# Seven of eight head groups put into one loop with register-based waits, in a decode-attention kernel that streams its cache

## Chip, cores, metric

One core of one Trainium2 chip. The metric is the device time of one execution in microseconds (us). The kernel before takes 1273.72 us (median of 3 runs, 1273.58 to 1274.66).

## The reference, cut to what matters

```python
# 16 query heads, 8 key/value heads, 65536 cached keys, head size 256, model width 448, bf16
g = sigmoid((x * gate_w).sum(-1, keepdims=True))
q = x @ wq                                            # one token
p = softmax((q @ k.T) * 256 ** -0.5)                  # two query heads share one K and V head
a = concat(p @ v) @ wo
b = gelu(layernorm(x)[:, None] * w1 + b1) @ w2 + b2   # the "mixer", 14 blocks of 128
out = g * a + (1 - g) * b
```

K and V are 268 MB each and are read once. Everything else is small. A *group* is one K/V head with its two query heads; there are eight.

## The kernel before, the parts that the change and the argument touch

A group is cut into six chunks of keys (6, 6, 5, 5, 5, 5 steps of 2048 keys). For each chunk one K load and one V load, of 5 or 6 MB, go into a ring of three slots. So the order of loads is K0, V0, K1, V1, ..., and a load waits until the slot of the third load before it is free. A K slot is free when VectorE has transposed it (`turn`); a V slot is free when TensorE has multiplied it (`p_v`).

```python
RING = 3
def load(item):                   # item 2*i is K of chunk i, 2*i+1 its V; i runs over all groups
    ...
    nc.sync.dma_start(out=ring[item % RING][...], in_=src[...])

n = 0
for i in range(total):            # total = 8 groups x 6 chunks, all unrolled
    g, c = divmod(i, n_chunks)
    for s in range(sizes[c]):
        turn(i, s, n)             # VectorE: transpose 2048 keys into kT (two buffers)
        scores(i, s, n)           # TensorE: 8 matmuls on kT
        mixer(n)                  # from step 4 on: one block per 8 steps, on ScalarE, POOL, TensorE
        if c == 0 and g > 0:      # the group before is finished inside the next one's first steps
            if s == 0: o_turn(g - 1) ...
            if s == 1: o_out(g - 1)
        n += 1
    load(2 * i + RING)            # into the K slot that turn has freed
    softmax(i)                    # ScalarE exp, VectorE transpose
    ...
    for s in range(...): p_v(i, s)
    load(2 * i + 1 + RING)        # into the V slot that p_v has freed
    if c == n_chunks - 1 and g + 1 < HKV:
        ...copy of pv; queries(g + 1)
# (cut) the tail: last chunk, output projection, store
```

The softmax here doesn't subtract the row's maximum and nothing guards it: scores larger than these inputs give would overflow.

## Time and profile before

| what | before |
|---|---|
| median time | 1273.72 us |
| DMA engines busy, slices at 90% or more | 39 of 40 |
| data moved | 545 MB, 429 GB/s on average |
| TensorE, VectorE busy | 58%, 49% |

The lines of the page of the kernel before: span, TensorE's busy time, the DMA engines' share and rate in 40 equal slices of the span, the DMA queues (packets, MB, share of 16 engines), and the loads (KB each, median us from issue to landing).

```profile
span 1271.5 us, 10502 instructions
PE 740.7 (58%) x4576; PEld 291.7 (23%) x4576; DVE 627.8 (49%) x388; ACT 58.4 (5%) x149; POOL 78.4 (6%) x145
...
DMA  9999999999999999999999999999999999999997
GB/s 409 424 428 434 432 437 431 430 433 432 434 428 436 433 433 432 431 435 431 432 432 432 435 432 432 433 430 435 433 430 436 432 432 432 434 426 439 435 426 308
...
q1 hardware_dynamic: 15416, 540.55, 98.6%
...
q8 instruction: 36, 0.59, 0.2%
...
ring<-in_A_k_cache_dram SPq DMA_DIRECT2D x31, 5120.0 KB, 30.0
ring<-in_A_v_cache_dram SPq DMA_DIRECT2D x31, 5120.0 KB, 23.5
```

The DMA engines are busy 90% or more in 39 of the 40 slices, so they are the limit. A 5 MB load needs about 12 us at 432 GB/s but lands 23.5 or 30.0 us after its issue: when it is issued, one to two others are still queued. Queue q8: 36 fetches of 16 KB of instructions.

The line of the table of waits (who waited, for whom, us in total, times, longest) that says the same from VectorE's side:

```profile
DVE kT L351 <- DMA ring<-in_A_k_cache_dram: 386.0, 46, 10.5
```

The boundary between groups seven and eight in the timeline (start, us, engine or issuing queue, line, operation, in brackets the idle time before it and who ended it): the K1 issue after the last p.v of group seven, VectorE's transposes of K0 of group eight, and the V1 issue that they free.

```profile
1120.18 0.33 SPq L97 DMA_DIRECT2D ring<-in_A_k_cache_dram  x1
...
1125.65 4.50 DVE L351 STREAM_TRANSPOSE kT<-ring 128x2048 f32<-128x2048 f32 x2 [8.16 <-DMA ring<-in_A_k_cache_dram]
...
1140.79 0.33 SPq L97 DMA_DIRECT2D ring<-in_A_v_cache_dram  x1
```

In the chain of waits, that K1 load and what it released:

```profile
1120.18 34.40 DMA ring<-in_A_k_cache_dram
...
1154.76 2.32 DVE kT L351
```

V1 is issued at 1140.8, while K1 is still landing until 1154.6: the queue is 14 us ahead.

### The profile page before, as it was taken

The numbers are of one execution on the slowest core, as the hardware profiler recorded it, in microseconds if no ns is written. First come the engines' busy times: TensorE is split into PE (matmuls) and PEld (weight loads), VectorE is DVE, ScalarE is ACT, GpSimd is POOL, SyncE is SP. The second block draws the span as 40 slices with busy tenths as digits, with TensorE's granted clock in tenths as the row PEclk, the third lists the DMA queues.
The fourth block names the chain that finished last, engine by engine and source line by source line (L and its number), as shares of the span: only waits on it lengthen the run. The fifth ranks groups of instructions, "written<-read, shape, count | busy, mean of one in ns | idle before, by whom it ended". The sixth has DMA issues, their size and how long they took to land.

```text
span 1271.5 us, 10502 instructions
## 1 busy us (share of the span) xinstructions
PE 740.7 (58%) x4576; PEld 291.7 (23%) x4576; DVE 627.8 (49%) x388; ACT 58.4 (5%) x149; POOL 78.4 (6%) x145
## 2 busy tenths in 40 slices
PE   1566556664566546665566646665466555665467
PEld 1222122221222212221222212222122211222123
DVE  2555354644545454553545445454454535544455
ACT  0000000000000000000000000000000000000000
POOL 4110101111011110110000000000000000000000
PEclk9878877887778877888778887788777887878889
DMA  9999999999999999999999999999999999999997
GB/s 409 424 428 434 432 437 431 430 433 432 434 428 436 433 433 432 431 435 431 432 432 432 435 432 432 433 430 435 433 430 436 432 432 432 434 426 439 435 426 308
DMA packets 16843, 544.92 MB, mean 429 GB/s; under 512 B 2202, under 2 KB 2332, under 8 KB 3484
## 3 DMA queue, kind: packets, MB, share of 16 engines
q1 hardware_dynamic: 15416, 540.55, 98.6%
q0 software_dynamic: 1376, 3.69, 0.8%
q8 instruction: 36, 0.59, 0.2%
q14 instruction: 11, 0.09, 0.0%
q10 hardware_dynamic: 4, 0.00, 0.0%
HBM read 544.22 MB, written 0.00 MB: 428 GB/s over the span
## 4 chain that ended last, share of the span: by engine, by line
DMA 62%; PE 19%; DVE 11%; issue 6%; ACT 1%; POOL 0%; DVEq 0%; ACTq 0%; SPq 0%; POOLq 0%
DMA ring<-in_A_k_cache_dram 59%; PE sc L359 14%; DVE kT L351 9%; PE pv L382 5%; DMA zb<-in_B_b_dram 2%; DMA ring<-in_A_v_cache_dram 1%; DVE pT L370 1%; ACT p L366 1%; PE den_ps L398 0%; PE misc L270 0%; PE acc L314 0%; DVEq L351 0%; PE misc L425 0%; PE misc L274 0%; DVE dsum L390 0%
## 5 line engine op out<-in xcount | busy, mean ns | idle before, releaser
L359 PE MATMUL sc<-kT,qw 128*128 128x512 bf16 x2048 | 587.8, 441 | 425.6 <-DVE kT L351 424.3
L351 DVE STREAM_TRANSPOSE kT<-ring 128x2048 f32<-128x2048 f32 x256 | 576.4, 2290 | 476.9 <-DMA ring<-in_A_k_cache_dram 386.0
L359 PEld LDWEIGHTS <-qw 128*128 128x128 bf16 x2048 | 218.9, 109 | 780.9 <-DVE kT L351 324.0
L382 PE MATMUL pv<-ring,pT 128*4 128x512 bf16 x2032 | 127.5, 401 | 61.8 <-DVE pT L370 61.8
L370 DVE STREAM_TRANSPOSE pT<-p 128x512 bf16<-128x512 bf16 x48 | 34.1, 711 | 130.9 <-ACT p L366 130.9
L382 PEld LDWEIGHTS <-pT 128*4 128x4 bf16 x2032 | 47.2, 90 | 136.3 <-DVE pT L370 81.7
L366 ACT ACTIVATE p<-sc 128x512 bf16<-128x512 f32 x48 | 28.7, 597 | 1035.1 <-PE sc L359 1035.1
L143 POOL DMA_DIRECT2D wo<-in_A_wo_dram x8 | 6.3, 790 | 552.5 <-PE acc L314 552.5
L333 POOL TENSOR_SCALAR t_b<-t_b 128x448 f32<-128x448 f32 x14 | 7.9, 564 | 224.9 <-ACT t_b L325 224.6
L336 POOL TENSOR_TENSOR t_b<-t_b,u_b 128x448 f32<-128x448 f32 x14 | 15.9, 1139 | 1.2
L343 POOL TENSOR_TENSOR gel<-t_b,u_b 128x448 bf16<-128x448 f32 x14 | 15.9, 1133 | 1.2
L339 POOL TENSOR_SCALAR t_b<-t_b,half_g 128x448 f32<-128x448 f32 x14 | 8.9, 636 | 106.4 <-ACT t_b L338 101.3
L414 PEld LDWEIGHTS misc<-sel,pvs 128*128 128x128 f32 x64 | 13.8, 299 | 3.6 <-issue 2.0
L414 PE MATMUL misc<-sel,pvs 128*128 128x2 f32 x64 | 12.2, 313 | 0.5 <-DVE pvs L472 0.5
L398 PE MATMUL den_ps<-pick,dsum 128*128 128x2 f32 x32 | 4.8, 256 | 12.5 <-DVE dsum L390 12.5
L227 PE MATMUL misc<-zb,one_f 1*128 1x2 f32 x2 | 0.6, 343 | 19.4 <-DMA zb<-in_B_b_dram 19.4
L325 ACT ACTIVATE t_b<-h_bc,b1T,w1T 128x448 f32<-128x448 f32 x14 | 10.5, 751 | 4.7 <-DVE h_bc L257 4.7
L329 POOL TENSOR_SCALAR u_b<-h_bc,w1T,b1T 128x448 f32<-128x448 f32 x14 | 10.0, 715 | 2.1 <-DVE qT L277 0.9
L366 ACT ACTIVATION_READ_ACCUMULATOR p<-sc 128x1 f32 x48 | 9.3, 194 | 0.0
L230 DVE TENSOR_SCALAR gate<-gate 128x2 f32<-128x2 f32 x1 | 0.2, 169 | 18.4 <-ACT gate L229 18.4
L164 POOL TENSOR_SCALAR_AFFINE_SELECT pick<-pick 128x2 f32<-128x2 f32 x44 | 8.5, 195 | 3.0 <-POOL pick L164 0.3
L338 ACT ACTIVATE t_b<-t_b 128x448 f32<-128x448 f32 x14 | 8.0, 572 | 13.4 <-POOL t_b L336 13.4
(75 smaller groups left out, 68.1 us busy)
## 6 DMA issues: line engine op xcount, KB each, us to landing
ring<-in_A_k_cache_dram SPq DMA_DIRECT2D x31, 5120.0 KB, 30.0
ring<-in_A_v_cache_dram SPq DMA_DIRECT2D x31, 5120.0 KB, 23.5
ring<-in_A_k_cache_dram SPq DMA_DIRECT2D x16, 6144.0 KB, 32.3
ring<-in_A_v_cache_dram SPq DMA_DIRECT2D x16, 6144.0 KB, 27.3
ring<-in_A_k_cache_dram SPq DMA_DIRECT2D x5, 1024.0 KB, 25.8
ring<-in_A_v_cache_dram SPq DMA_DIRECT2D x4, 1024.0 KB, 22.0
wo<-in_A_wo_dram POOLq DMA_DIRECT2D x8, 448.0 KB, 18.8
ring<-in_A_wq_dram SPq DMA_DIRECT2D x1, 3072.0 KB, 10.3
```

The lines of the kernel that those rows point to most:

```text
L164: nc.gpsimd.affine_select(out=t, in_=t, compare_op=ALU.not_equal, fill=1.0, base=-row, pattern=[[step, w]], channel_multiplier=1,)
L325: nc.scalar.activation(out=t_b[:], in_=h_bc[:], func=ACT.Square, scale=w1T[:, b:b + 1], bias=b1T[:, b:b + 1],)
L329: nc.gpsimd.tensor_scalar(out=u_b[:], in0=h_bc[:], scalar1=w1T[:, b:b + 1], scalar2=b1T[:, b:b + 1], op0=ALU.mult, op1=ALU.add,)
L336: nc.gpsimd.tensor_tensor(out=t_b[:], in0=t_b[:], in1=u_b[:], op=ALU.mult)
L339: nc.gpsimd.tensor_scalar(out=t_b[:], in0=t_b[:], scalar1=1.0, scalar2=half_g[:, 0:1], op0=ALU.add, op1=ALU.mult,)
L343: nc.gpsimd.tensor_tensor(out=gel[:], in0=t_b[:], in1=u_b[:], op=ALU.mult)
L351: nc.vector.transpose(out=kT[n % 2][:].bitcast(FP32), in_=kn[:, s * SB * 128:(s + 1) * SB * 128])
L359: nc.tensor.matmul(sc[i % 2][:], lhsT=qw[g % 2][:, q, PAD - s:PAD - s + 128], rhs=kv[:, :, q // 2, :, q % 2], start=(s == 0 and q == 0), s ...
L366: nc.scalar.activation(out=p_t[i % 2][:], in_=sc[i % 2][:], func=ACT.Exp, scale=scale, accum_out=den[g % 2][:, c:c + 1],)
L370: nc.vector.transpose(out=pT_t[i % 2][:], in_=p_t[i % 2][:])
L382: nc.tensor.matmul(pv[g % 2][32 * a:32 * a + 4, :], lhsT=pT[:, k, :, s], rhs=vt[:, j * DH:(j + 2) * DH], start=first and k < 4, stop=last ...
L414: nc.tensor.matmul(o_ps[:, 2 * c:2 * c + 2], lhsT=pvs[:, lo:lo + 128], rhs=sel[:, 2 * half:2 * half + 2], start=(half == 0 and c == 0), st ...
```

## The change

The intent: the eight groups are the same work, so seven become the body of one loop (a seventh of that code) and the eighth, with the special tail, stays unrolled. `iteration_sync="reg_based"` is chosen so that no barrier stands between passes. A group is finished at its own end and no longer inside the next one, `pv`, `den`, `qw` and `wo_t` need one buffer each, and the mixer moves into group eight, with two product buffers and a block per one and a half steps.

```diff
-    n = 0
-    for i in range(total):
-        g, c = divmod(i, n_chunks)
-        for s in range(sizes[c]):
-            turn(i, s, n)
-            scores(i, s, n)
-            mixer(n)
-            if c == 0 and g > 0:
-                ... (o_turn, o_out of the group before)
+    def group(g):
+        final = g is HKV - 1
+        n = 0
+        for i in range(n_chunks):
+            ends = i == n_chunks - 1
+            for s in range(sizes[i]):
+                turn(i, s, n)
+                scores(i, s, n)
+                if final:
+                    mixer(n)
+                n += 1
+            load(g, 2 * i + RING)        # items 12, 13, 14 are K0, V0, K1 of group g + 1
+            softmax(i)
+            ... den_sum, den_tot, p_v as before
+            load(g, 2 * i + 1 + RING)
+        if not final:
+            queries(g + 1)
+            nc.scalar.activation(out=pvs[:], in_=pv[:], func=ACT.Copy)
+            o_turn(); ...; o_out()
+            load_wo(g + 1)
+
+    with tc.For_i(0, HKV - 1, 1, iteration_sync="reg_based") as g:
+        group(g)
+    group(HKV - 1)
```

(The cut parts of the diff only pass `g` as a register into addresses and drop the double buffers.) The diff does not show what the built program does: at the loop's *exit*, SyncE waits 34.4 us, until the last load that the loop has issued has landed, and then all engines meet at a barrier before group eight: TensorE, VectorE, ScalarE and GpSimd all start on it between 1151.1 and 1151.3 us, after 32 to 40 us idle (parts of the trace are below).

More of the change, by code (lines that the diff above doesn't have):

```diff
@@ L64 @@
     n_chunks = len(sizes)
-    n_steps = HKV * sum(sizes)
+    n_items = 2 * n_chunks
+    assert n_items % RING == 0 and n_chunks % 2 == 0 and sum(sizes) % 2 == 0 and n_items > RING + 2
     scale = 1.0 / (DH ** 0.5)
@@ L80 @@
     sc = [psum.tile([128, 512], FP32, name=f"sc{i}") for i in range(2)]
-    pv = [psum.tile([128, 512], FP32, name=f"pv{i}") for i in range(2)]
+    pv = psum.tile([128, 512], FP32, name="pv")
     misc = psum.tile([128, 512], FP32, name="misc")
@@ L85, with piece @@
     acc = psum.tile([128, 512], FP32, name="acc")
-    total = HKV * n_chunks
-    def piece(item, j, n):
+    def piece(g, item, j, n):
         i, is_v = divmod(item, 2)
-        g, c = divmod(i, n_chunks)
-        nb = sizes[c] * SB
-        lo = sum(sizes[:c]) * SB * 128
-        src = (A_v_cache if is_v else A_k_cache)[0, g, lo:lo + 128 * nb, :]
-        src = src.rearrange("(p j) d -> p (j d)", j=nb)
+        nb = sizes[i] * SB
+        lo = sum(sizes[:i]) * SB * 128
+        src = (A_v_cache if is_v else A_k_cache)[0, bass.ds(g, 1), lo:lo + 128 * nb, :]
+        src = src.rearrange("o (p j) d -> p (o j d)", j=nb)
         nc.sync.dma_start(
@@ L99, in piece, with load @@
         )
-    def load(item):
+    def load(g, item):
         last = sizes[-1]
-        if item < 2 * total - 2:
-            piece(item, 0, sizes[item // 2 % n_chunks] * SB)
-        elif item == 2 * total - 1:
+        if item >= n_items:
+            if g is not HKV - 1:
+                load(g + 1, item - n_items)
+        elif g is not HKV - 1 or item < n_items - 2:
+            piece(g, item, 0, sizes[item // 2] * SB)
+        elif item == n_items - 1:
             for s in range(last):
-                piece(item - 1, s * SB, SB)
+                piece(g, item - 1, s * SB, SB)
             for s in range(last - 1):
-                piece(item, s * SB, SB)
-            piece(item, (last - 1) * SB, SB - TAIL)
-            piece(item, last * SB - TAIL, TAIL)
+                piece(g, item, s * SB, SB)
+            piece(g, item, (last - 1) * SB, SB - TAIL)
+            piece(g, item, last * SB - TAIL, TAIL)
     wq_slot = ring[RING - 1]
@@ L123 @@
     for item in range(RING - 1):
-        load(item)
+        load(0, item)
     x_row = const.tile([1, D], BF16)
@@ L138 @@
     nc.gpsimd.dma_start(out=zb[:, 1:2], in_=B_b2.rearrange("(o n) -> o n", o=1))
-    wo_t = [const.tile([128, 4, D], BF16, name=f"wo{i}") for i in range(2)]
+    wo_t = const.tile([128, 4, D], BF16)
     def load_wo(g):
-        nc.gpsimd.dma_start(
-            out=wo_t[g % 2][:],
-            in_=A_wo[g * 512:(g + 1) * 512, :].rearrange("(q p) n -> p q n", p=128),
-        )
+        src = A_wo.rearrange("(g q p) n -> p g q n", q=4, p=128)[:, bass.ds(g, 1)]
+        nc.gpsimd.dma_start(out=wo_t[:], in_=src.rearrange("p o q n -> p (o q) n"))
     ident = const.tile([128, 128], BF16)
@@ L185 @@
     pT_t = [work.tile([128, 512], BF16, name=f"pT{i}") for i in range(2)]
-    den = [work.tile([128, n_chunks], FP32, name=f"den{i}") for i in range(2)]
+    den = work.tile([128, n_chunks], FP32, name="den")
     dsum = work.tile([128, len(classes)], FP32, name="dsum")
@@ L195 @@
     qr = const.tile([128, 8, HQ], BF16)
-    qw = [const.tile([128, 8, WIN], BF16, name=f"qw{i}") for i in range(2)]
+    qw = const.tile([128, 8, WIN], BF16)
     gate = const.tile([128, 2], FP32)
-    for t in pv + qw:
+    for t in (pv, qw):
         nc.vector.memset(t[:], 0.0)
@@ L291, in queries @@
         for r in range(2):
-            h = 2 * g + r
             cols = slice(PAD + 16 * r, PAD + 16 * r + 97, 32)
             nc.vector.tensor_tensor(
-                out=qw[g % 2][:, :, cols], in0=qr[:, :, h:h + 1].to_broadcast([128, 8, 4]),
+                out=qw[:, :, cols], in0=qr[:, :, bass.ds(2 * g + r, 1)].to_broadcast([128, 8, 4]),
                 in1=block[:].rearrange("p (o a) -> p o a", o=1).to_broadcast([128, 8, 4]),
@@ L300, with to_acc @@
     queries(0)
-    load(RING - 1)
+    load(0, RING - 1)
     load_wo(0)
-    load_wo(1)
     t_b = work.tile([128, D], FP32, name="t_b")
-    gel = work.tile([128, D], BF16, name="gel")
-    MIX = min(8, (n_steps - 4) // (NF + 1))
-    opened = set()
-    def to_acc(col, rows, stop=False):
+    gel = [work.tile([128, D], BF16, name=f"gel{i}") for i in range(2)]
+    def to_acc(col, rows):
         for a in range(4):
@@ L315, in to_acc, with mix @@
                 acc[32 * a:32 * a + 1, 0:DQ], lhsT=col, rhs=rows[:, DQ * a:DQ * (a + 1)],
-                start=a not in opened, stop=stop, tile_position=(0, 32 * a),
+                start=False, stop=False, tile_position=(0, 32 * a), skip_group_check=True,
             )
-            opened.add(a)
     def mixer(n):
-        b, ph = divmod(n - 4, MIX)
-        if not 0 <= b < NF:
-            return
+        for b in range(NF):
+            ph = n - 3 * b // 2
+            mix(b, ph)
+    def mix(b, ph):
         if ph == 0:
@@ L336, in mixer @@
             nc.gpsimd.tensor_tensor(out=t_b[:], in0=t_b[:], in1=u_b[:], op=ALU.mult)
-        if ph == 2:
+        if ph == 1:
             nc.scalar.activation(out=t_b[:], in_=t_b[:], func=ACT.Tanh, scale=GELU_C0)
@@ L342, in mixer @@
             )
-            nc.gpsimd.tensor_tensor(out=gel[:], in0=t_b[:], in1=u_b[:], op=ALU.mult)
-        if ph == 5:
-            to_acc(w2T[:, b:b + 1], gel[:])
+            nc.gpsimd.tensor_tensor(out=gel[b % 2][:], in0=t_b[:], in1=u_b[:], op=ALU.mult)
+        if ph == 4:
+            to_acc(w2T[:, b:b + 1], gel[b % 2][:])
     def turn(i, s, n):
@@ L355, in scores @@
     def scores(i, s, n):
-        g, c = divmod(i, n_chunks)
         kv = kT[n % 2][:].rearrange("p (j b y two) -> p j b y two", j=SB, b=4, two=2)
@@ L359, in scores, with p_v @@
             nc.tensor.matmul(
-                sc[i % 2][:], lhsT=qw[g % 2][:, q, PAD - s:PAD - s + 128], rhs=kv[:, :, q // 2, :, q % 2],
-                start=(s == 0 and q == 0), stop=(s == sizes[c] - 1 and q == 7),
+                sc[i % 2][:], lhsT=qw[:, q, PAD - s:PAD - s + 128], rhs=kv[:, :, q // 2, :, q % 2],
+                start=(s == 0 and q == 0), stop=(s == sizes[i] - 1 and q == 7),
             )
     def softmax(i):
-        g, c = divmod(i, n_chunks)
         nc.scalar.activation(
             out=p_t[i % 2][:], in_=sc[i % 2][:], func=ACT.Exp, scale=scale,
-            accum_out=den[g % 2][:, c:c + 1],
+            accum_out=den[:, i:i + 1],
         )
         nc.vector.transpose(out=pT_t[i % 2][:], in_=p_t[i % 2][:])
-    def p_v(i, s):
-        g, c = divmod(i, n_chunks)
+    def p_v(i, s, last):
         vt = ring[(2 * i + 1) % RING]
         pT = pT_t[i % 2][:].rearrange("p (i b x) -> p i b x", b=4, x=16)
-        first = c == 0 and s == 0
-        last = (g, c, s) == (HKV - 1, n_chunks - 1, sizes[c] - 3)
-        last |= g < HKV - 1 and c == n_chunks - 1 and s == sizes[c] - 1
+        first = i == 0 and s == 0
         for k in range(SB // 2):
@@ L382, in p_v, with den_sum @@
             nc.tensor.matmul(
-                pv[g % 2][32 * a:32 * a + 4, :], lhsT=pT[:, k, :, s], rhs=vt[:, j * DH:(j + 2) * DH],
+                pv[32 * a:32 * a + 4, :], lhsT=pT[:, k, :, s], rhs=vt[:, j * DH:(j + 2) * DH],
                 start=first and k < 4, stop=last and k >= SB // 2 - 4, tile_position=(0, 32 * a),
             )
-    def den_sum(g):
+    def den_sum():
         for k, size in enumerate(classes):
@@ L390, in den_sum, with den_tot @@
             nc.vector.tensor_reduce(
-                out=dsum[:, k:k + 1], in_=den[g % 2][:, lo:lo + sizes.count(size)], axis=AXIS.X,
+                out=dsum[:, k:k + 1], in_=den[:, lo:lo + sizes.count(size)], axis=AXIS.X,
                 op=ALU.add,
             )
-    def den_tot(g):
+    def den_tot():
         for k in range(len(classes)):
@@ L407, with o_turn @@
     o_ps = misc[:, 504:508]
-    def o_turn(g):
+    def o_turn():
         for half in range(2):
@@ L428, in p_v_turned, with o_out @@
                 )
-    def o_out(g):
+    def o_out():
         for c in range(2):
             for r in range(2):
-                to_acc(
-                    oT[:, 2 * c + r:2 * c + r + 1], wo_t[g % 2][:, 2 * r + c, :],
-                    stop=(g == HKV - 1 and c == 1 and r == 1),
-                )
-        if g + 2 < HKV:
-            load_wo(g + 2)
-    n = 0
-    for i in range(total):
-        g, c = divmod(i, n_chunks)
-        for s in range(sizes[c]):
-            turn(i, s, n)
-            scores(i, s, n)
-            mixer(n)
-            if c == 0 and g > 0:
-                if s == 0:
-                    o_turn(g - 1)
-                    for r in range(2):
-                        nc.scalar.activation(
-                            out=oT[:, r:4:2], in_=o_ps[:, r:4:2], func=ACT.Copy, scale=rden[:, r:r + 1]
-                        )
-                if s == 1:
-                    o_out(g - 1)
-            n += 1
-        if 2 * i + RING < 2 * total:
-            load(2 * i + RING)
-        softmax(i)
-        if c == n_chunks - 1:
-            den_sum(g)
-            den_tot(g)
-        for s in range(sizes[c] - 2 * (i == total - 1)):
-            p_v(i, s)
-        if 2 * i + 1 + RING < 2 * total:
-            load(2 * i + 1 + RING)
-        if c == n_chunks - 1 and g + 1 < HKV:
-            nc.scalar.activation(out=pvs[:], in_=pv[g % 2][:], func=ACT.Copy)
-            queries(g + 1)
@@ L471 @@
-    g, i, s = HKV - 1, total - 1, sizes[-1] - 1
-    nc.vector.tensor_copy(out=pvs[:, 0:DH], in_=pv[g % 2][:, 0:DH])
-    nc.scalar.activation(out=pvs[:, DH:2 * DH], in_=pv[g % 2][:, DH:2 * DH], func=ACT.Copy)
-    o_turn(g)
+                to_acc(oT[:, 2 * c + r:2 * c + r + 1], wo_t[:, 2 * r + c, :])
+    def group(g):
[11 more added lines that the diff above has]
+            softmax(i)
+            if ends:
+                den_sum()
+                den_tot()
+            steps = sizes[i] - 2 * (final and ends)
+            for s in range(steps):
+                p_v(i, s, ends and s == steps - 1)
+            load(g, 2 * i + 1 + RING)
+        if not final:
+            queries(g + 1)
+            nc.scalar.activation(out=pvs[:], in_=pv[:], func=ACT.Copy)
+            o_turn()
+            for r in range(2):
+                nc.scalar.activation(
+                    out=oT[:, r:4:2], in_=o_ps[:, r:4:2], func=ACT.Copy, scale=rden[:, r:r + 1]
+                )
+            o_out()
+            load_wo(g + 1)
@@ L475 @@
+    with tc.For_i(0, HKV - 1, 1, iteration_sync="reg_based") as g:
+        group(g)
+    group(HKV - 1)
+    i, s = n_chunks - 1, sizes[-1] - 1
+    nc.vector.tensor_copy(out=pvs[:, 0:DH], in_=pv[:, 0:DH])
+    nc.scalar.activation(out=pvs[:, DH:2 * DH], in_=pv[:, DH:2 * DH], func=ACT.Copy)
+    o_turn()
     p_v_turned(i, s - 1, 0, SB)
@@ L481 @@
     )
-    o_out(g)
+    o_out()
     nc.vector.tensor_scalar(
```

## The prediction

> **What bounds the kernel now.** The transfers. On the page, the 16 DMA engines are 90% or more busy in 39 of 40 slices and move 429 GB/s on average, 545 MB in all; VectorE is busy 49%, TensorE 58%. In the table of waits VectorE waits 386 us for K chunks to land. At each issue one to two chunks are still queued: 5 MB K chunks land 30.0 us after issue, V chunks 23.5 us, and one alone takes about 12 us at 432 GB/s. So an issue may come 11 to 17 us late before the DMA engines run dry, and only dry time costs anything.
>
> **What the change does** (from the program order):
>
> 1. Back edges (six). No barrier; a few register instructions, a branch and a jump back. [...] A group's output turn now stands ahead of the next group's scores: copy 0.6, turn 1.0, scaling 0.4, output matmuls 0.4 us, with hand-overs about 4 us. At the boundary at 1120 us in the timeline the next K lands 5.5 us after the last p.v, so TensorE idles then anyway, and the V issue at 1140.8 us had 14 us to spare before the last queued chunk landed at 1154.6. Expected: at most 1 us each.
>
> 2. The loop's exit (one). SyncE waits there for every transfer issued in the loop, then an all-engine barrier stands ahead of group eight. In flight are its K0, V0, K1. Until K1 has landed nobody may transpose K0, so no slot comes free and no issue can follow. From the same boundary: last p.v to K1 landed 34.4 us; [...]six transposes of K0 until the V1 issue 15.1 us[...]. The DMA engines stand still for about 19 us, wholly on the critical path; nothing wins it back, because before and after the hole they run full.
>
> 3. The mixer moves from the first 120 steps to the first 23 of group eight. A block takes 5.2 us in the timeline at 77 us. ScalarE's order puts the first softmax behind the fourth block's Tanh: 19 us after the barrier, where scores would be done at 17; the second at about 41. I estimate the K3 issue at 45 to 50 us, with the queue full until about 56. No second hole, or 1 to 2 us.
>
> Removed: most of the instruction stream, at most 0.7 MB of fetches, 0 to 1.5 us. Prologue and tail stay.
>
> **Sum.** 1273.7 + 19 (exit) + 0 to 3 (back edges, mixer) - 0 to 1.5 (fetches): 1293 us, 1.5% slower. Range 1285 to 1304. Chances: faster by over 2% 0.02, within 2% 0.77, slower by over 2% 0.21.
>
> **What would show it.** Step 1: GB/s stays near 430 in every slice of the loop. Step 2: one slice at about 1140 to 1175 us loses about 60% of its DMA share; SyncE waits for a K transfer there; VectorE's first transpose of group eight starts about 36 us after the last p.v of group seven instead of 5.5, and the V1 issue 15 us later. Step 3: softmax waits behind ScalarE's Tanh, and the DMA share recovers by the next slice.
>
> **What would make it wrong.** If a back edge starves an engine of instructions for over 14 us, each iteration opens a hole: slower by over 2%. If the mixer delays the K3 issue more, a second hole of 5 to 10 us follows. If the exit does not wait for K1, the time stays at 1274. If instruction fetches slow the queues more than their bytes say, it gains a few us.

The forecast came to 1293 us: 1273.7 + 19 for the exit + 0 to 3 for back edges and mixer - 0 to 1.5 for fetches. Terms are cut out of it: of the 19 us, two of about 2 us each (barrier and branch; issue to first bytes) were derived from no figure of the trace, and the 15.1 us of transposes remain. Step 1: the step's "at most 1 us each" was my estimate.

## The result

The changed kernel is correct and takes 1288.63 us (median of 4 runs, 1287.31 to 1289.55); the kernel before takes 1274.19 us beside it. The ratio is 1.0112, with a 95% interval of 1.0094 to 1.0129. Ratios here are the mean time of one kernel's runs over that of the other's of the same rounds, so not quite the ratio of the medians.

The same lines of the page of the changed kernel:

```profile
span 1287.3 us, 11599 instructions
PE 725.7 (56%) x4576; PEld 285.6 (22%) x4576; DVE 625.1 (49%) x386; ACT 60.3 (5%) x149; POOL 78.2 (6%) x145
...
DMA  9999999999999999999999999999999999967997
GB/s 407 429 427 433 434 431 440 428 434 429 441 430 433 429 437 434 433 430 439 433 430 432 438 434 436 433 430 434 429 437 436 431 429 439 431 286 312 428 429 331
...
q1 hardware_dynamic: 15416, 540.55, 97.3%
...
q8 instruction: 10, 0.16, 0.0%
...
ring<-in_A_k_cache_dram SPq DMA_DIRECT2D x31, 5120.0 KB, 29.4
ring<-in_A_v_cache_dram SPq DMA_DIRECT2D x31, 5120.0 KB, 23.4
```

Two slices, at 286 and 312 GB/s, hold the loss. A slice is 32.2 us; against 434 GB/s they lack (1 - 286/434) x 32.2 + (1 - 312/434) x 32.2 = 20 us. No slice inside the loop dips, and the fetches of instructions fell from 36 to 10.

VectorE's wait for K, and SyncE's wait at the loop's exit, from the tables of waits:

```profile
DVE kT L347 <- DMA ring<-in_A_k_cache_dram: 361.9, 43, 11.8
```

```profile
SPq L457 <- DMA ring<-in_A_k_cache_dram: 34.4, 1, 34.4
```

The boundary between groups seven and eight again:

```profile
1114.71 0.33 SPq L96 DMA_DIRECT2D ring<-in_A_k_cache_dram  x1
...
1151.14 4.50 DVE L347 STREAM_TRANSPOSE kT<-ring 128x2048 f32<-128x2048 f32 x2 [39.72 <-PEq L504]
...
1166.44 0.35 SPq L96 DMA_DIRECT2D ring<-in_A_v_cache_dram  x1
...
1170.82 0.58 ACT L360 ACTIVATE p<-sc 128x512 bf16<-128x512 f32 x1
...
1176.36 0.34 SPq L96 DMA_DIRECT2D ring<-in_A_k_cache_dram  x1
...
1202.40 0.33 SPq L96 DMA_DIRECT2D ring<-in_A_k_cache_dram  x1
```

And busy times in stretches of that hole (from:to in us, its length, then each engine's busy us, the granted clock, the DMA engines' share, GB/s):

```profile
1145.00:1147.00 2.00, 0.00 (x0) 0.00 (x0) 0.00 (x0) 0.00 (x0) 0.00 (x0) 0.50 0.91 393
1147.00:1148.00 1.00, 0.00 (x0) 0.00 (x0) 0.00 (x0) 0.00 (x0) 0.00 (x0) 0.50 0.46 197
1148.00:1150.00 2.00, 0.00 (x0) 0.00 (x0) 0.00 (x0) 0.00 (x0) 0.00 (x0) 0.50 0.00 0
1150.00:1166.00 16.00, 11.53 (x40) 4.45 (x40) 13.10 (x6) 4.01 (x6) 11.42 (x14) 0.73 0.01 3
1166.00:1168.00 2.00, 1.85 (x13) 0.86 (x12) 0.42 (x1) 0.34 (x1) 1.40 (x2) 1.00 1.25 369
```

These stretches count a packet where it starts: the last ones start shortly before 1148. The load K1 counts as landed 35.4 us after its issue in the profile's table of loads, at 1150.1. The first transpose after the barrier starts at 1151.14, 36.4 us after the K1 issue instead of 5.5; V1 is issued 15.3 us after that, and packets start again from about 1167. So none starts for about 19.5 us, and the slices lack 20 us.

There is a second difference, of the other sign. The last load of the loop is issued at 1114.71 instead of 1120.18: by this measure the changed kernel is 5.5 us *ahead* by the end of the loop. At the output's issue it is 15.6 us behind (1284.35 against 1268.77). So by issue times the two profiled runs split as -5.5 inside the loop and +21.1 from the exit to the end. The experiments test both terms.

An issue time is an elastic measure, since a load may be issued some microseconds sooner or later while the queue is full. Counted from the packets of the traces, the first 480 MB of the load queue (q1) have landed 4.0 us sooner than in the kernel before. Of these, 1.2 us are already there after the first 50 MB.

### The profile page after: what moved, and what is told of

The parts are those of the page before. It is cut to its first block, busy times and chain, and to the rows that moved or that the text cites. A ratio compares the mean times of both kernels' runs of the same rounds, so it can differ in the third digit from the quotient of the medians.

```text
span 1287.3 us, 11599 instructions
## 1 busy us (share of the span) xinstructions
PE 725.7 (56%) x4576; PEld 285.6 (22%) x4576; DVE 625.1 (49%) x386; ACT 60.3 (5%) x149; POOL 78.2 (6%) x145
## 5 line engine op out<-in xcount | busy, mean ns | idle before, releaser
L354 PE MATMUL sc<-kT,qw 128*128 128x512 bf16 x2048 | 569.2, 431 | 433.0 <-DVE kT L347 431.9
L354 PEld LDWEIGHTS <-qw 128*128 128x128 bf16 x2048 | 215.9, 107 | 779.7 <-issue 372.8
L373 PE MATMUL pv<-ring,pT 128*4 128x512 bf16 x2032 | 130.4, 408 | 74.8 <-DVE pT L364 74.5
L146 POOL DMA_DIRECT2D wo_t<-in_A_wo_dram x8 | 6.1, 762 | 1084.7 <-PE L354 927.8
L332 POOL TENSOR_TENSOR t_b<-t_b,u_b 128x448 f32<-128x448 f32 x14 | 15.9, 1134 | 1.2
L405 PE MATMUL misc<-sel,pvs 128*128 128x2 f32 x64 | 9.2, 266 | 7.4 <-ACT pvs L448 6.8
L405 PEld LDWEIGHTS misc<-sel,pvs 128*128 128x128 f32 x64 | 8.6, 208 | 12.8 <-ACT pvs L448 11.6
L389 PEld LDWEIGHTS den_ps<-pick,dsum 128*128 128x128 f32 x32 | 4.3, 188 | 16.9 <-issue 14.8
```

Source lines behind the costliest of these rows:

```text
L332: nc.gpsimd.tensor_tensor(out=t_b[:], in0=t_b[:], in1=u_b[:], op=ALU.mult)
L354: nc.tensor.matmul(sc[i % 2][:], lhsT=qw[:, q, PAD - s:PAD - s + 128], rhs=kv[:, :, q // 2, :, q % 2], start=(s == 0 and q == 0), stop=(s ...
L373: nc.tensor.matmul(pv[32 * a:32 * a + 4, :], lhsT=pT[:, k, :, s], rhs=vt[:, j * DH:(j + 2) * DH], start=first and k < 4, stop=last and k > ...
L389: nc.tensor.matmul(den_ps[:, 0:2], lhsT=dsum[:, k:k + 1].to_broadcast([128, 128]), rhs=pick[:, :, k], start=(k == 0), stop=(k == len(class ...
L405: nc.tensor.matmul(o_ps[:, 2 * c:2 * c + 2], lhsT=pvs[:, lo:lo + 128], rhs=sel[:, 2 * half:2 * half + 2], start=(half == 0 and c == 0), st ...
```

## The experiments

Eleven kernels ran. All are edits of the changed kernel. "Before" beside each means the kernel before on the same chip in the same rounds.

My theory: (a) the exit drains the load queue, and because K0 can be transposed only behind the barrier, the hole is 15 us of transposes plus about 5 us of landing, barrier, issue and first bytes; (b) inside the loop the gain comes from fewer instruction fetches, which the profile lists among the packets of the same DMA engines (queue q8). Rivals: the back edges, the mixer in group eight, or the barrier itself carry the loss; the new order or the single buffers carry the gain.

### unrolled: the new order without the loop

```diff
-    with tc.For_i(0, HKV - 1, 1, iteration_sync="reg_based") as g:
-        group(g)
-    group(HKV - 1)
+    for g in range(HKV):
+        group(g)
```

> The body of the changed kernel with a plain unrolled repetition in place of the loop: same order within a group, mixer in group eight, one pv bank, but no loop exit and no back edge. My theory (the exit's drained queue costs about 20 us; the 5.5 us gained inside the loop come from fewer instruction fetches on the DMA engines, 10 against 36 packets of 16 KB): fetches back at about 36 and the time at that of before, 1274 (1272 to 1276). Rival A (the new order of the group end, or the single buffers, gained the 5.5 us): 1268.5. Rival B (the mixer in the last group is what costs): 1280 or more.

Measured: correct, 1273.09 us (before 1273.37); ratio 0.9999, interval 0.9985 to 1.0012. The line of its page on instruction fetches:

```profile
q8 instruction: 36, 0.59, 0.2%
```

So the new order, the single buffers and the mixer's move cost and gain nothing in sum, within about 1.5 us. The loss belongs to the loop. Of the gain, a part belongs to the order: in its profiled run the same load of the boundary is issued at 1118.43, 1.75 us earlier than in the kernel before, and by the data that have landed unrolled has the 1.2 us of the first 50 MB too. Against unrolled, the changed kernel has the first 480 MB 2.3 us sooner; that is what is left for the loop.

### two_loops: one exit more

```diff
-    with tc.For_i(0, HKV - 1, 1, iteration_sync="reg_based") as g:
-        group(g)
+    with tc.For_i(0, 4, 1, iteration_sync="reg_based") as g:
+        group(g)
+    with tc.For_i(4, HKV - 1, 1, iteration_sync="reg_based") as g:
+        group(g)
     group(HKV - 1)
```

> The seven groups in two loops of four and three, so one exit more and one back edge less; doubles the suspected cost. My theory: a second hole in the DMA share of about 20 us at the end of group four, 1309 us (1305 to 1312). Rival (back edges or the mixer carry the cost, or the hole belongs to the last group alone): 1287 to 1291.

Measured: correct, 1313.58 us (before 1273.37); ratio 1.0309, interval 1.0295 to 1.0323. SyncE's waits at the two exits, and the rate by slices:

```profile
SPq L459 <- DMA ring<-in_A_k_cache_dram: 34.9, 1, 34.9
SPq L457 <- DMA ring<-in_A_k_cache_dram: 34.4, 1, 34.4
```

```profile
GB/s 400 436 429 431 433 434 429 438 436 434 434 430 432 433 439 432 430 436 433 435 312 246 427 437 430 441 428 437 425 445 426 430 437 437 433 305 291 438 425 320
```

A second hole appears where the second exit is, and the time grows by 25 us over the changed kernel. An exit is what costs. My figure of 20 us was 5 too small for this one, and the time lies just above the range I gave: its first transpose starts 40.6 us after the K1 issue (646.46 to 687.04) instead of 36.4, so the restart takes some 4 us more here. The load lands as before, 35.5 us after its issue; the 4 us lie between landing and first transpose. In that gap the trace shows three packets of instruction fetches (684.5 to 686.0 us). Whether they fill the 4 us was not tested.

### rotated: the exit where a slot is already free

The body is turned round so that the next group's first transposes and scores stand at its end. At the exit K0 is already done, and the first thing after the barrier is the V1 issue. Barrier and wait are the same.

```diff
-        n = 0
+        n = sizes[0]
         for i in range(n_chunks):
             ends = i == n_chunks - 1
-            for s in range(sizes[i]):
+            for s in range(sizes[i] * (i > 0)):
                 turn(i, s, n)
                 scores(i, s, n)
                 if final:
-                    mixer(n)
+                    mixer(n - sizes[0])
...
             o_out()
             load_wo(g + 1)
+            first_scores()
+
+    def first_scores():
+        for s in range(sizes[0]):
+            turn(0, s, s)
+            scores(0, s, s)
+
+    first_scores()
```

> The loop's body is rotated: K0's transposes and scores of the next group stand at the end of the body, so that at the exit slot 0 is already free and V1's load is the first thing issued after the barrier. Same barrier, same wait for all transfers. My theory (the hole is the 15 us of K0's transposes behind the barrier, plus about 5 us of landing, barrier, issue and first bytes): 1273 us (1271 to 1276), with a hole of about 5 us. Rival (the barrier and the restart of the engines themselves cost most of it): 1284 or more.

Measured: correct, 1281.24 us (before 1273.37); ratio 1.0059, interval 1.0045 to 1.0072. Neither theory's number. Its stretches around the exit:

```profile
1146.00:1148.00 2.00, 0.00 (x0) 0.00 (x0) 0.00 (x0) 0.00 (x0) 0.00 (x0) 0.50 0.57 246
1148.00:1150.00 2.00, 0.00 (x0) 0.00 (x0) 0.00 (x0) 0.00 (x0) 0.00 (x0) 0.50 0.00 0
1150.00:1152.00 2.00, 0.00 (x0) 0.00 (x0) 0.18 (x1) 0.90 (x3) 0.71 (x1) 0.50 0.00 0
1152.00:1154.00 2.00, 1.41 (x16) 0.53 (x20) 2.00 (x2) 0.44 (x1) 1.39 (x2) 0.50 1.23 377
```

The hole is the 5 us that the theory asks for (no packet starts from about 1147.2 to 1152). The rest of the loss is elsewhere, in the tail. In its timeline, the last scores of the fifth chunk and the softmax that follows them:

```profile
1243.45 1.90 PE L354 MATMUL sc<-kT,qw 128*128 128x512 bf16 x8
...
1251.85 0.58 ACT L360 ACTIVATE p<-sc 128x512 bf16<-128x512 f32 x1
...
1252.56 0.71 DVE L364 STREAM_TRANSPOSE pT<-p 128x512 bf16<-128x512 bf16 x1 [9.15 <-ACT p L360]
```

The scores end at 1245.4, the softmax starts at 1251.85: ScalarE takes its work in order here: its timeline shows three of the mixer's blocks (first operation at 1238.20, 1243.46 and 1248.69, the last Tanh at 1251.37) and only then the softmax. Group eight has six steps less for the mixer in this version, so the mixer now ends in the sixth chunk. VectorE waits 9.15 us for that softmax, the last chunk is late by as much, and it is the tail, where no load is left to hide it.

### no_mixer: the changed kernel without the mixer

```diff
-                if final:
-                    mixer(n)
```

> The changed kernel without the mixer (a wrong result on purpose): nothing else changes. My theory: the mixer's waits in group eight are hidden, because the next load is issued while the first is still moving; 1288.5 us (1287 to 1290). Rival (the mixer's chain behind the barrier deepens the hole): 1280 to 1286.

Measured: wrong (relative error 0.90), 1287.81 us (before 1273.37); ratio 1.0111, interval 1.0096 to 1.0127. The same as with the mixer. In the changed kernel the mixer costs nothing that these runs resolve (the intervals are about 2 us either way); the hole is the exit's.

### rotated_no_mixer and rotated_pace: is the tail of rotated the mixer's?

```diff
 (rotated_no_mixer, on rotated)
-                if final:
-                    mixer(n - sizes[0])
 (rotated_pace, on rotated)
-            ph = n - 3 * b // 2
+            ph = n - b
```

> The rotated kernel without the mixer (a wrong result on purpose). Theory as for rotated_pace: 1273 us (1271 to 1274.5), 8 us less than rotated. Rival (the tail of rotated is late for another reason than the mixer): still about 1281.

> The rotated kernel with one mixer block per step in place of two per three steps, so that the mixer ends in the second step of the fifth chunk instead of in the sixth chunk. Theory (the rotated kernel's hole is the 5 us expected, and the other 8 us are the tail: softmax of the fifth chunk waited behind the mixer on ScalarE and the last chunk ended 8 us late): 1273 us (1271.5 to 1275), correct result, last transfer about 5 us before the end as in the kernel before. Rival (the tail is late for another reason): still about 1281.

Measured: rotated_no_mixer, wrong, 1273.54 us (before 1273.48), ratio 0.9998. rotated_pace 1272.97 us, ratio 0.9996, but its result is *wrong* (relative error 0.34): with two product buffers and one block per step, the product of a block was overwritten by the block after next before TensorE read it. Its time is therefore no proof of a usable kernel. rotated_no_mixer alone shows that the 8 us were the mixer's.

### rotated_pace2 and rotated_gel6: a correct version of it

```diff
 (rotated_pace2, on rotated_pace)
-        if ph == 4:
+        if ph == 3:
             to_acc(w2T[:, b:b + 1], gel[b % 2][:])
 (rotated_gel6, on rotated_pace)
-    gel = [work.tile([128, D], BF16, name=f"gel{i}") for i in range(2)]
+    gel = [work.tile([128, D], BF16, name=f"gel{i}") for i in range(6)]
...                                     (the product is written to gel[b % 6] too)
-        if ph == 4:
-            to_acc(w2T[:, b:b + 1], gel[b % 2][:])
+        if ph == 6:
+            to_acc(w2T[:, b:b + 1], gel[b % 6][:])
```

> rotated_pace gave a wrong result, because a block's product was overwritten by the block after next before TensorE had read it: at one block per step the matmul must stand three steps after the block's start, not four. This run mends that and changes nothing else. Expected: correct, 1273 us (1271.5 to 1275) as rotated_pace: the loop's 5.5 us gained and the exit's 5 us lost cancel, so it ties with the kernel before. If it is under 1270 the hole is smaller than I read; if it is about 1281 the tail is not cured by the pace.

Measured: correct, 1277.95 us (before 1273.69); ratio 1.0033, interval 1.0019 to 1.0047. A miss of 5 us. Now the mixer's products wait for TensorE's matmuls, the third softmax of group eight starts at 1210.0 us, and the K load behind it is issued only at 1215.6, when the queue has just run dry. That dip is the smaller part of the miss: against rotated_gel6 below, the last data land 1 us later, but the fourth softmax starts at 1232.6 instead of 1223.7 and the run ends 4.7 us later. So it is again the tail's own work that waits behind the mixer.

> rotated_pace2 was 5 us above rotated_pace: with two product buffers and one block per step the mixer's products waited for TensorE's matmuls, the third softmax of group eight waited behind them until 1210 us, and the K load behind it was issued too late (the transfers dip at 1216 us). Here six product buffers let the mixer run ahead freely, one block per step, matmul six steps later. Expected: correct, third softmax at about 1204 us, no dip, 1273 us (1271.5 to 1274.5), a tie with the kernel before. Rival (more than the mixer's own order holds the tail): 1277 or more.

Measured: correct, 1273.26 us (before 1273.39); ratio 0.9998, interval 0.9984 to 1.0011. With free product buffers the third softmax starts at 1205.4, and of the slices before the tail only the exit's is low. Its rate by slices and fetches:

```profile
GB/s 409 425 432 433 433 431 430 437 434 433 435 430 434 434 433 432 434 433 434 435 435 430 434 433 434 429 437 434 433 431 435 433 434 433 435 435 360 433 429 335
...
q8 instruction: 10, 0.16, 0.1%
```

This is the best loop version found: 15 us under the changed kernel, level with the kernel before. The gain from the loop and the hole of 5 us at the exit cancel.

### body_1500, body_2300, body_busy: what do instruction fetches cost?

After each chunk of the loop's body come `N` small matmuls into a PSUM tile that nobody reads.

```diff
             load(g, 2 * i + 1 + RING)
+            for _ in range(N * (not final)):
+                nc.tensor.matmul(
+                    dump[0:1, 0:W], lhsT=ident[:, 0:1], rhs=R, start=True, stop=True
+                )
 body_1500: N = 32,  W = 1,   R = ident[:, 0:1]       1500 TensorE instructions in the body
 body_2300: N = 100, W = 1,   R = ident[:, 0:1]       2316
 body_busy: N = 40,  W = 256, R = pairs[:, 0, :]      1596
```

> The changed kernel with 32 idle one-element matmuls after each chunk of the loop's body: TensorE's body grows from 1116 to 1500 instructions. Control for the next run. Theory (a body that is fetched once costs no fetches in later passes): about 12 instruction packets of 16 KB, 1288.5 us (1287 to 1290.5). Rival (TensorE's extra work delays the transfers): 1292 or more.

> The same with 100 such matmuls after each chunk: 2316 TensorE instructions in the body[...]. Theory (the 5 us that the loop gained come from fetches that no longer go through the same DMA engines as the data, about 0.15 to 0.2 us each): the body is fetched again in each pass, 60 to 75 packets of 16 KB, and the time grows by 8 to 12 us over body_1500, to about 1298. Rival A (fetches cost the data stream nothing, the gain has another cause): the same as body_1500 within 1.5 us although the packets are there. Rival B (a missed back edge stalls an engine long enough to open holes): 1310 or more, with dips in the DMA share at the loop's boundaries.

(That this body would be fetched again in each pass was my assumption, and this run tests it.)

> Control for body_2300: 40 idle matmuls of 256 columns after each chunk, so that TensorE is kept busy about as long as by the 100 short ones (about 5 us a chunk), but the body has only 1596 instructions. Theory (the fetches cost body_2300 its 14 us): about 12 instruction packets and 1288 us (1287 to 1290). Rival (TensorE's extra work, not the fetches, made body_2300 slow): 1298 or more.

Measured, all correct: body_1500 1288.06 us (before 1273.48), body_2300 1301.96 us (before 1273.48, ratio 1.0221, interval 1.0207 to 1.0235), body_busy 1288.46 us (before 1273.69). TensorE's line and the instruction queue of body_2300, rate by slices between them:

```profile
PE 936.7 (72%) x8776; PEld 491.6 (38%) x8776; DVE 625.5 (48%) x386; ACT 60.3 (5%) x149; POOL 78.1 (6%) x145
...
GB/s 404 426 431 438 426 438 427 436 425 438 430 434 426 438 432 428 430 438 425 440 423 437 423 430 433 425 431 429 416 431 431 424 430 421 429 254 310 427 431 317
...
q8 instruction: 76, 1.25, 0.4%
```

and those of body_busy:

```profile
PE 893.8 (69%) x6256; PEld 422.8 (33%) x6256; DVE 624.6 (49%) x386; ACT 60.3 (5%) x149; POOL 78.4 (6%) x145
...
q8 instruction: 12, 0.20, 0.1%
```

body_1500 has 12 packets too. So bodies of 1116, 1500 and 1596 TensorE instructions (my counts; the trace of the changed kernel shows 1134 in a pass) go with 10, 12 and 12 packets of 16 KB in the whole run, and in the changed kernel none of them starts between 122.8 and 1152.2 us, over six back edges. The body of 2316 goes with 76: 64 more than body_1500, on average about 11 for each of the six further passes. body_busy keeps TensorE almost as busy as body_2300 (894 against 937 us) and costs nothing over body_1500; body_2300 has 64 packets more and costs 13.9 us more, without a hole at any back edge. Nor does a late issue explain it: between 180 and 1110 us the DMA engines' share is 1.00 as in the changed kernel, but they move 430 instead of 433 GB/s. So it is the fetches: 13.9 / 64 = 0.22 us each, over my range of 0.15 to 0.20.

Not all of it is spread over the loop. In the profiled runs body_2300 has the first 490 MB 10.1 us later than body_1500, but its last data before the exit 13.2 us later. The stretches in which the queue drains at the exit show the difference; body_2300 first, then body_1500:

```profile
1154.00:1156.00 2.00, 0.00 (x0) 0.00 (x0) 0.00 (x0) 0.00 (x0) 0.00 (x0) 0.50 0.57 246
1156.00:1158.00 2.00, 0.00 (x0) 0.00 (x0) 0.00 (x0) 0.00 (x0) 0.00 (x0) 0.50 0.45 197
1158.00:1160.00 2.00, 0.00 (x0) 0.00 (x0) 0.00 (x0) 0.00 (x0) 0.00 (x0) 0.50 0.45 197
1160.00:1162.00 2.00, 0.00 (x0) 0.00 (x0) 0.00 (x0) 0.00 (x0) 0.00 (x0) 0.50 0.34 147
```

```profile
1146.00:1148.00 2.00, 0.00 (x0) 0.00 (x0) 0.00 (x0) 0.00 (x0) 0.00 (x0) 0.50 0.74 319
1148.00:1150.00 2.00, 0.00 (x0) 0.00 (x0) 0.00 (x0) 0.00 (x0) 0.00 (x0) 0.50 0.06 25
```

In body_1500, and in body_busy likewise, all engines end within about 3 us. In body_2300 about half of them still work on the last load for some 4 us when the others are done (8 packets under way from 1156.5 to 1160.5, where 16 is usual). The kernel before, with its 36 fetches, ends in the same way: in the last 6 us of its loads (1260 to 1266) the DMA share is 0.52, after 1.00 in the 6 us before, and its last 1.5 MB take 6.5 us. In the changed kernel they take 4.2 us. So the loop's gain has two parts: against unrolled, which also needs 6.5 us, 2.3 us of lead at the loop's end and 2.3 us in the last 1.5 MB. If all of it is due to the 26 fetches that are saved, that is 4.6 us, or 0.18 us each; body_2300's 0.22 would give 5.6. That this equals the 5.5 us of the issue times is a coincidence.

What stays open is why a fetch costs about 0.2 us. In the trace a 16 KB fetch is one packet of 0.97 us (35.0 us for 36 in the kernel before, which the page gives as 0.2% of the span of 16 engines). Spread evenly that would be 0.06 us of all engines' time; gathered on half of them, 0.12 us (my estimates from these figures). The uneven end suggests that the fetches do gather: body_2300's last load counts as landed at 1163.6, with its very last packets (1163.2), so late engines make the whole load late. But the trace does not name the engine that a packet ran on, so this is an inference, and it does not give the whole 0.2 us.

## Why the prediction was right, and where a term was off

- **What bounds the kernel.** Right. 168 us more TensorE work changed nothing (body_busy: 893.8 against 725.7 us busy); the time grew where the DMA engines stood still, where they also had to fetch instructions, and in the tail, where no load is left to hide a wait.
- **Back edges, "at most 1 us each".** Right as far as it shows: TensorE's idle time ahead of the first weights of the next pass is 0.7 to 0.8 us at each of the six, no slice of the loop dips, and the loop gained time as a whole. Even body_2300, with 64 fetches more than body_1500 over six further passes, shows no hole at a back edge.
- **The exit, "about 19 us".** Right in mechanism and size. K1 landed 35.4 us after its issue (34.4 forecast), landing to the first transpose took 1.0 us, the transposes to the V1 issue 15.3 us (15.1 forecast), and packets started about 1 us after the V1 issue. (Besides the transposes the forecast of 19 held some 4 us for barrier and first bytes, which it did not derive from any figure. The two took 2 us; the other 2 are the time from the last packets' start to their load's landing.) No packet starts for about 19.5 us; two_loops doubles the hole, rotated shrinks it to 5 us by taking the transposes out from behind the barrier.
- **The mixer, "no second hole, or 1 to 2 us".** Right for this kernel: no_mixer takes the same time. The first softmax came 19.7 us after the barrier (19 forecast), the K3 issue at 51 us (45 to 50 forecast, so a little late, but no slice dips). What I had not seen is how the mixer's pace holds up ScalarE's softmax once group eight has fewer steps for it: in rotated that cost 8 us. At the faster pace with two product buffers (rotated_pace2) it cost 5 us; whether the buffers also matter at rotated's own pace was not tested.
- **Instruction fetches, "at most 0.7 MB of fetches, 0 to 1.5 us".** This is the mis-sized term. I costed fetches by their bytes (0.5 MB at 430 GB/s is 1.2 us). They cost about 0.2 us per 16 KB packet, which makes some 5 us for the 26 that are saved. The net change was +14.4 us by the medians: 20 us of hole less about 5 us of fetches, where I had forecast 19 plus 0 to 3 less 0 to 1.5. With the 0 to 3 us allowed for back edges and mixer, of which nothing showed, this makes up the difference between 1293 and 1288.6. The forecast had named the case itself: fetches that "slow the queues more than their bytes say".

## What to carry to other kernels

This loop has no barrier on its back edges, but one at its exit, behind a wait of 34.4 us for the transfers in flight; in a kernel that lives from a queue that never runs dry, ask what must happen between that barrier and the next issue, and move it in front of the barrier (here 20 us became 5). The 16 KB fetches of instructions cost more here than their bytes say (0.2 against 0.04 us at 430 GB/s): count them, and measure one with a body long enough to bring more of them (here 2316 TensorE instructions brought 64 more than 1500, and 1596 none). Measure a lead by the data that have landed and not by when a load was issued; while the queue is full, an early issue gains nothing (body_1500 issues the last load of the loop 1.5 us before the changed kernel does, at 1113.24, and it lands no sooner, after 37.2 us instead of 35.4). And when work moves next to the tail, ask which engine now has it ahead of the tail's own work (here ScalarE, 8 us in rotated).
